# A planned step order, start-up work, the r selection and the weight layout of a one-core recurrence + MLP kernel

## Chip, cores and metric

The kernel runs on one core of one Trainium2 chip. The metric is device time of one execution in microseconds (us), lower is better; the time before is the median of three runs, 318.76 us (314.11 to 320.25).

## What is computed

A linear recurrence over 768 tokens for 4 batches x 8 heads with a 40 x 40 state each, then a two-layer MLP on the 3072 tokens (320 = 8 heads x 40):

```python
for t in range(S):                                   # S = 768, per batch and head
    y[:, :, t] = np.einsum('bhd,bhde->bhe', rt, state)
    Sa = np.einsum('bhde,bhe->bhd', state, at)
    state = state * wt[:, :, None, :] - np.einsum('bhd,bhe->bhde', Sa, bt) \
            + np.einsum('bhd,bhe->bhde', vt, kt)
x = y.transpose(0, 2, 1, 3).reshape(B * S, H * D)    # 3072 x 320
out = np.maximum(x @ w_in, 0.0) ** 2 @ w_out         # 320 -> 2048 -> 320
```

## The kernel before

The recurrence is taken in chunks of L = 64 tokens. A *group* g is one chunk of one pair of batches, so there are 12 x 2 = 24 groups of 128 rows (2 batches x 64 tokens) by 320 columns (8 heads x 40, often padded to 64 each). Group g needs the state that group g - 2 left, so two chains run interleaved. Everything is written in steps; each step is one or several instructions on one engine. A group's steps, with the names that the profile's tiles carry:

- Loads on SP (L289, L302): W, K, B, A, V each as two DMAs of 64 x 8 x 40 floats, R as one DMA of 128 rows of 1280 bytes. Three buffers of each.
- Decay sums: LN (ACT, LNW), LO (POOL, LLO, the low half of a split in two bf16), CS and CE (PE, L323, L336, L340), EXN and EXE (ACT), GLM (POOL).
- Scaling: KBS0, KBS1 (POOL, KB), AS (POOL, A), RC (POOL, RB, a cast of r), VC0, VC1 (POOL, VM, a cast of v into two of four blocks) and VZ0, VZ1 (POOL memsets of the other two).
- Transposes on PE with a copy out of PSUM: KT/KTE (L384, L388), AT/ATE (L394, L406), RT/RTE (L401, L410). RT is the *r selection*: r comes in as rows of eight tokens, and 16 matmuls against pieces of the identity put token u of each eight into every eighth PSUM column.
- The chunk: EB and its mask EBE (DVE, L433), XV + X0 (x, L444, L452), the negated copies UA, UB (ACT, UZ, L457), COR (L466), MA, MB (ACT, VM, L471), the state update ST, STE, SX, SXE (L481 to L504), VT, VTE (L511, L515), CP, CPE (L429, L433), YC + YS (y, L525, L533), YE (DVE).
- The MLP: XT, XTE (transpose), then for each half of the 2048 hidden units U (L561, 64-row matmuls for the last 64 of the 320 inputs), UX and UY (L570) into one PSUM tile hp, RL (ACT relu, L575), SQ (DVE square, L579, tile GT), and down-projections D0 to D3 (L588, tile fo), OE (ACT, L593), OST (SP, two stores of 64 rows, L599).

`Plan` (L37) sets the order. It is a list scheduler at build time: every step has an engine, a guessed duration, dependencies, a shape `mode` on PE (R: 64- or 40-row operands, M: whole 128 x 128, C: 64-column outputs) and a place `g * PERIOD + PLACE[name]`. At each turn it takes, over the engines, the step that can start first; among the steps of an engine that could start within a small window, the one with the lowest place, PE steps of another mode getting a malus of 1.5. Instructions are then issued engine by engine in that order, and on the chip each engine works its own queue in order. PSUM is handed out in the plan: three one-bank buffers S, one two-bank buffer each D (cs, eb, cp) and HP (both halves hp0, hp1), one F (fo).

The constants (identity ID, triangles TI, TE, MASK, selectors SELB, BM, I2) and the zero pads are written ahead of all steps: DVE and POOL memset whole tiles. The weights are loaded by four POOL DMAs with a cast to bf16, ahead of all steps on POOL: WIN as 2 x 128 rows and 128 rows from 192 on (so that input rows 192 to 255 are there twice), WOUT as rows of 320 floats:

```python
nc.gpsimd.dma_start(out=V(WOUT, 0, [(DM, 16), (1, DM)]),
                    in_=moe_w_out.rearrange("(j p) f -> p j f", p=128))
```

Hidden unit 128 * blk + p is thus column p of block blk, a contiguous 128 columns of WIN.

Of the kernel before, what the change touches and what calls it, by code (L numbers as in the profile page):

```python
# [7 lines left out]
FP32 = mybir.dt.float32  # L8
# [6 lines left out]
PERIOD = 9.3  # L15
PLACE = {
# [10 lines left out]
}  # L27
SWITCH = 0.1
# [3 lines left out]
class Op:  # L32
    __slots__ = ("name", "g", "eng", "dur", "fn", "deps", "mode", "alloc", "frees", "place",
# [3 lines left out]
class Plan:  # L37


    LAG = {"PE": 0.2, "ACT": 0.15, "DVE": 0.15, "POOL": 0.2, "SP": 2.2}  # L40
# [14 lines left out]
    def run(self):  # L55
# [19 lines left out]
        while left:  # L75
            best = None
            for e, cand in avail.items():
                lst = []
                for o in cand:
                    t = max(free[e], o.ready)  # L80
                    if o.alloc:
                        cls, key = o.alloc
                        if (key, o.g) not in held:
                            fr = [x for x in banks[cls] if x is not None]
                            if not fr:
                                continue
                            t = max(t, min(fr))
# [11 lines left out]
            if best is None:  # L99
                raise RuntimeError("no step can start")  # L100
# [37 lines left out]
def kernel(  # L138
# [97 lines left out]
    for t in LNW + LLO + A + RB:  # L236
        nc.gpsimd.memset(t[:], 0.0)
# [400 lines left out]
```

## Time and profile before

| | |
|---|---|
| median of three runs | 318.76 us (314.11 to 320.25) |
| the profiled execution | 317.43 us, of which span 315.7 us |
| PE / its weight loads (PEld) | 271.5 us (86%) / 216.9 us (69%) busy |
| DVE / ACT / POOL | 186.9 (59%) / 149.6 (47%) / 142.4 us (45%) busy |
| DMA | 31.29 MB, mean 99 GB/s; loads and stores 49.5%, weights 5.5% of 16 engines' span |
| chain that ended last | PE 70%, SP's queue 11%, DVE 6%, ACT 5% |
| granted TensorE clock | 0.987 |

The span is the time from the first to the last instruction; the execution's own time has 1.7 us around it. A row of a group view names line, engine, operation, output tile <- input tiles and shape, then busy time and mean ns of one instruction, then idle time of the engine before it and what ended that. A row of a timeline gives start and length in us, then the instruction; in brackets stands how long the engine had been idle and for whom. Matmuls are pipelined and overlap, so their mean ns is not the time that one costs. PEld is the load of the stationary operand, which runs beside the matmuls. DMA rows give the median time from issue to landing.

### The profile page before, as it was taken

To read this page: it belongs to the slowest core of one execution; us is meant where nothing else is said; L and a number is where in the kernel's file an instruction comes from. 1 tells how busy PE (TensorE), PEld (TensorE's weight loads), DVE (VectorE), ACT (ScalarE), POOL (GpSimd) and SP (SyncE) were. 2 spreads that over 40 slices of the span, in tenths; PEclk is the share of its full clock that TensorE was granted. 3 is DMA by queue.
4 is the path that set the end of the run, shared out by engine and by line. 5 is a ranking of instruction groups with operands and counts; after the bars stand their busy time and mean duration, and the time that the engine had idled before them with its cause. 6 is when DMAs were issued, how large, how long until landed. Compare 5 with 4: busy or idle time off the path is not lost.

```text
span 315.7 us, 13625 instructions
## 1 busy us (share of the span) xinstructions
PE 271.5 (86%) x5928; PEld 216.9 (69%) x5928; DVE 186.9 (59%) x288; ACT 149.6 (47%) x265; POOL 142.4 (45%) x259
## 2 busy tenths in 40 slices
PE   0132899599999899999999999999999999999872
PEld 0031678478787578777878778887887787787651
DVE  7420538545583585587566577758665855875620
ACT  2103254255737445665455654565456465453431
POOL 8442576433755354646345733456444562510000
PEclk9999999989999799999999999999999999999999
DMA  5999776677665766666665765657564311001110
GB/s 80 196 182 167 119 119 110 121 111 142 116 141 87 128 121 106 113 129 124 101 119 108 116 125 99 117 100 125 106 117 89 55 36 23 22 5 23 23 23 21
DMA packets 136571, 31.29 MB, mean 99 GB/s; under 512 B 127936, under 2 KB 136128, under 8 KB 136512
## 3 DMA queue, kind: packets, MB, share of 16 engines
q1 hardware_dynamic: 134016, 27.55, 49.5%
q0 software_dynamic: 2496, 2.88, 5.5%
q8 instruction: 46, 0.75, 1.0%
q14 instruction: 13, 0.11, 0.1%
HBM read 29.36 MB, written 3.93 MB: 105 GB/s over the span
## 4 chain that ended last, share of the span: by engine, by line
PE 70%; SPq 11%; DVE 6%; ACT 5%; DMA 3%; issue 3%; POOL 0%; ACTq 0%; POOLq 0%
PE fo L588 17%; PE hp L570 15%; SPq L289 10%; PE hp L561 5%; PE sx L500 3%; PE vt L511 3%; PE kt L384 3%; PE rt L401 3%; DVE GT L579 3%; PE cs L323 2%; PE y L525 2%; ACT RL L575 2%; DMA Wf<-in_w_dram 2%; PE st L481 2%; PE x L444 2%
## 5 line engine op out<-in xcount | busy, mean ns | idle before, releaser
L575 ACT ACTIVATE RL<-hp 128x1024 bf16<-128x1024 f32 x48 | 49.1, 1023 | 63.7 <-PE hp L570 60.8
L588 PE MATMUL fo<-WOUT,GT 128*128 128x320 bf16 x384 | 61.5, 303 | 3.5 <-DVE GT L579 3.1
L356 POOL TENSOR_TENSOR KB<-KBf,EXN 128x320 bf16<-128x320 f32 x48 | 40.8, 870 | 35.6 <-issue 12.3
L570 PE MATMUL hp<-XT,WIN 128*128 128x128 bf16 x768 | 54.4, 223 | 0.0
L570 PEld LDWEIGHTS <-WIN 128*128 128x128 bf16 x768 | 45.4, 100 | 5.6 <-issue 0.4
L588 PEld LDWEIGHTS <-GT 128*128 128x128 bf16 x384 | 34.8, 99 | 17.3 <-DVE GT L579 5.1
L579 DVE TENSOR_TENSOR GT<-RL 128x1024 bf16<-128x1024 bf16 x48 | 37.7, 785 | 12.5 <-ACT RL L575 12.2
L362 POOL TENSOR_TENSOR A<-Af,EXE 128x320 bf16<-128x320 f32 x24 | 20.9, 869 | 38.2 <-issue 21.8
L372 POOL CAST VM<-Vf 64x320 bf16<-64x320 f32 x48 | 23.2, 483 | 27.1 <-issue 15.5
L433 DVE TENSOR_TENSOR CPM<-cp,MASK 128x1024 bf16<-128x1024 f32 x24 | 29.2, 1216 | 4.5 <-PE cp L429 4.5
L433 DVE TENSOR_TENSOR EBM<-eb,MASK 128x1024 bf16<-128x1024 f32 x24 | 29.2, 1217 | 3.2 <-PE eb L429 3.1
L515 DVE COPY VMT<-vt 128x1024 bf16<-128x1024 bf16 x24 | 16.5, 689 | 24.3 <-PE vt L511 24.1
L457 ACT ACTIVATE UZ<-x 64x320 bf16<-64x320 f32 x48 | 20.6, 430 | 13.5 <-PE x L452 13.0
L388 DVE COPY KBT<-kt 128x1024 bf16<-128x1024 bf16 x24 | 16.5, 687 | 15.7 <-PE kt L384 15.5
L329 ACT ACTIVATE EXN<-cs 128x640 f32<-128x640 f32 x24 | 16.8, 700 | 14.6 <-PE cs L323 13.9
L367 POOL CAST RB<-Rf 128x320 bf16<-128x320 f32 x24 | 11.3, 470 | 27.0 <-PE rt L401 11.5
L471 ACT ACTIVATE VM<-x 64x320 bf16<-64x320 f32 x48 | 20.6, 429 | 5.7 <-PE x L466 5.2
L561 PE MATMUL hp<-XT,WIN 64*128 64x128 bf16 x384 | 19.4, 221 | 3.5 <-ACT RL L575 2.2
L315 POOL TENSOR_TENSOR LLO<-LNW 128x320 bf16<-128x320 f32 x24 | 17.8, 742 | 9.1 <-ACT LNW L307 8.4
L406 DVE COPY ART<-ar 128x512 bf16<-128x512 bf16 x24 | 10.0, 419 | 19.2 <-PE ar L394 19.1
L593 ACT ACTIVATE OSB<-fo 128x320 f32<-128x320 f32 x24 | 10.5, 436 | 22.2 <-PE fo L588 22.1
L307 ACT ACTIVATE LNW<-Wf 128x320 f32<-128x320 f32 x24 | 11.2, 466 | 20.1 <-DMA Wf<-in_w_dram 20.0
(81 smaller groups left out, 500.5 us busy)
## 6 DMA issues: line engine op xcount, KB each, us to landing
Wf<-in_w_dram SPq DMA_DIRECT2D x48, 80.0 KB, 3.1
KBf<-in_k_dram SPq DMA_DIRECT2D x48, 80.0 KB, 3.1
KBf<-in_b_dram SPq DMA_DIRECT2D x48, 80.0 KB, 3.2
Af<-in_a_dram SPq DMA_DIRECT2D x48, 80.0 KB, 3.0
Rf<-in_r_dram SPq DMA_DIRECT2D x24, 160.0 KB, 3.4
Vf<-in_v_dram SPq DMA_DIRECT2D x48, 80.0 KB, 3.1
out_dram<-OSB SPq DMA_DIRECT2D x48, 80.0 KB, 2.5
WIN<-in_moe_w_in_dram POOLq DMA_DIRECT2D x3, 512.0 KB, 8.1
```

The source lines that it names most:

```text
L289: nc.sync.dma_start(out=V(dst, off(be), [(40, 8), (1, 40)], 64 * h, 64), in_=tok(src, b0 + be))
L356: nc.gpsimd.tensor_tensor(out=V(kb, 512 * be, [(64, 8), (1, 40)]), in0=V(kbf, 320 * be, [(40, 8), (1, 40)]), in1=V(exn, 320 * be, [(40, 8) ...
L362: nc.gpsimd.tensor_tensor(out=V(at, 0, [(64, 8), (1, 40)]), in0=V(af, 0, [(40, 8), (1, 40)]), in1=V(exe, 0, [(40, 8), (1, 40)]), op=ALU.mult)
L372: nc.gpsimd.tensor_copy(out=V(vm, 512 * be, [(64, 8), (1, 40)], h, 64), in_=V(vf, 0, [(40, 8), (1, 40)], h, 64))
L433: nc.vector.tensor_tensor(out=V(dst, 0, [(64, 16), (1, 64)]), in0=V(psum(key, g), 0, [(64, 16), (1, 64)]), in1=V(MASK, 0, [(0, 16), (1, 64 ...
L457: nc.scalar.activation(out=V(uz, 320 * be, [(1, 320)], 64 * be, 64), in_=V(psum("x", g), 0, [(1, 320)], 64 * be, 64), func=ACTF.Copy, scal ...
L471: nc.scalar.activation(out=V(vm, 512 * be, [(64, 8), (1, 40)], 64 * be, 64), in_=V(psum("x", g), 0, [(40, 8), (1, 40)], 64 * be, 64), func ...
L561: mm(out=V(p, 512 * s + 128 * i, [(1, 128)]), lhsT=WIN[1 + s][64 * s:64 * s + 64, 128 * blk:128 * blk + 128], rhs=xt[64 * s:64 * s + 64, 1 ...
L570: mm(out=V(p, 512 * s + 128 * i, [(1, 128)]), lhsT=WIN[x][:, 128 * blk:128 * blk + 128], rhs=xt[:, 128 * x:128 * x + 128], start=False, st ...
L575: nc.scalar.activation(out=rl[:], in_=psum(f"hp{hf}", g)[:], func=ACTF.Relu)
L579: nc.vector.tensor_tensor(out=gt[:], in0=rl[:], in1=rl[:], op=ALU.mult)
L588: mm(out=p[:, 0:320], lhsT=gt[:, 512 * s + 128 * i:512 * s + 128 * i + 128], rhs=WOUT[:, DM * blk:DM * blk + DM], start=blk == 0, stop=blk ...
```

## The change

Six things are altered; every matmul and every elementwise result stays as it was.

1. *Order.* `PLACE`, `PERIOD`, `SWITCH`, the durations and the lags are other numbers; the first three and last three groups get offsets of their own. The malus for changing the PE shape is `STAY`, almost three periods, and the window is 0.11 for PE and zero for the other engines.
2. *Constants and pads as steps.* The constants, the ACT table load and the zero pads are steps that the plan places. Only the pads are zeroed where the rest is written anyway, on DVE. VZ is left out for the first three groups, whose VM is zeroed whole.
3. *First group.* K and B of group 0 are issued from ACT's queue, its KBS1 runs on DVE.
4. *r selection.* The 16 matmuls write 64 contiguous PSUM columns each, against a reordered identity SEL; the copy RTE reads PSUM with a step of 64 columns instead.
5. *Weights.* POOL's weight DMAs are steps after AS of group 0. WOUT row p holds hidden units 16p to 16p + 15 (20 KB of floats, in two DMAs); accordingly the blocks of WIN are read as every sixteenth column. WIN[2] gets 64 rows by DMA and 64 by a DVE copy from WIN[1].
6. *Store.* One DMA of 128 rows per group.

```diff
-PERIOD = 9.3
+PERIOD = 68.08
 PLACE = {
-    "LW": -40, "LK": -39, "LB": -38.5, "LA": -38, "LR": -37, "LV": -36,
...
+    "EB": -15.21, "LW": -4.79, "CS": -4.71, "OE": -1.57, "LB": -0.39, "UY0": -0.07, "MASK": 2.65, "RL1": 2.77,
...
-SWITCH = 0.1
+FIRST = {
...
+LAST = {
...
+SWITCH = 0.095
+STAY = 192.14
+WINDOW = {"PE": 0.11, "ACT": 0, "DVE": 0, "POOL": 0, "SP": 0}
...
-        o.place = g * PERIOD + PLACE[name]
+        o.place = g * PERIOD + PLACE[name] + (FIRST.get(name, 0) if g < 3 else LAST.get(name, 0) if g >= 21 else 0)
...
-                t0 = min(x[0] for x in lst)
-                d = 0.2 if e == "PE" else 0.05
-                t, o = min((x for x in lst if x[0] <= t0 + d),
-                           key=lambda x: (x[1].place + (1.5 if e == "PE" and x[1].mode != mode else 0), x[1].seq))
+                lim = min(x[0] for x in lst) + WINDOW[e]
+                t, o = min((x for x in lst if x[0] <= lim),
+                           key=lambda x: (x[1].place + (STAY if e == "PE" and x[1].mode != mode else 0), x[1].seq))
...
-    for t in LNW + LLO + A + RB:
-        nc.gpsimd.memset(t[:], 0.0)
-    for t in KB + UZ + STB + VM:
-        nc.vector.memset(t[:], 0.0)
...
+            eng = "ACT" if g == 0 and name in ("LK", "LB") else "SP"
+            q_ = nc.scalar if eng == "ACT" else nc.sync
...
-                nc.gpsimd.tensor_tensor(
+                (nc.vector if g == 0 and be else nc.gpsimd).tensor_tensor(
                     out=V(kb, 512 * be, [(64, 8), (1, 40)]), in0=V(kbf, 320 * be, [(40, 8), (1, 40)]),
...
-                    mm(out=V(p, u, [(64, 8), (8, 8)], 64 * al, 64), lhsT=rb[:, 64 * u:64 * u + 64],
-                       rhs=V(ID, 8 * al, [(16, 4), (64, 2), (1, 8)]), start=True, stop=True)
+                    mm(out=V(p, 64 * u, [(1, 64)], 64 * al, 64), lhsT=rb[:, 64 * u:64 * u + 64],
+                       rhs=SEL[:, 64 * al:64 * al + 64], start=True, stop=True)
...
-            nc.scalar.activation(out=art[:, 512:1024], in_=psum("rt", g)[:], func=ACTF.Copy)
+            nc.scalar.activation(out=V(art, 512, [(8, 64), (1, 8)]), in_=V(psum("rt", g), 0, [(1, 64), (64, 8)]),
+                                 func=ACTF.Copy)
...
-                        mm(out=V(p, 512 * s + 128 * i, [(1, 128)]), lhsT=WIN[1 + s][64 * s:64 * s + 64, 128 * blk:128 * blk + 128],
+                        mm(out=V(p, 512 * s + 128 * i, [(1, 128)]), lhsT=V(WIN[1 + s], blk, [(16, 128)], 64 * s, 64),
...
-                            mm(out=V(p, 512 * s + 128 * i, [(1, 128)]), lhsT=WIN[x][:, 128 * blk:128 * blk + 128],
+                            mm(out=V(p, 512 * s + 128 * i, [(1, 128)]), lhsT=V(WIN[x], blk, [(16, 128)]),
...
-            for be in range(2):
-                r0 = (b0 + be) * T + c * L
-                nc.sync.dma_start(out=out[r0:r0 + L, :], in_=osb[64 * be:64 * be + 64, :])
-        add("OST", g, "SP", (2, 0.4), f, [("OE", g)])
+            dst = out[b0 * T + c * L:b0 * T + c * L + L, :]
+            dst = bass.AP(dst.tensor, dst.offset, [[T * DM, 2], [DM, L], [1, DM]])
+            nc.sync.dma_start(out=dst, in_=osb[:])
+        add("OST", g, "SP", 0.6, f, [("OE", g)], dma=0.7)
...
+    def pads(t, n):
+        return V(t, 40, [(64, n), (1, 24)])
+    for i in range(2):
+        init(f"zL{i}", "DVE", 0.2, lambda i=i: (nc.vector.memset(pads(LNW[i], 8), 0.0), nc.vector.memset(pads(LLO[i], 8), 0.0)))
...
+    for i, (r0, n, p0) in enumerate(((0, 128, 0), (128, 128, 0), (256, 64, 64))):
+        init(f"wi{i}", "POOL", 0.6, lambda i=i, r0=r0, n=n, p0=p0: nc.gpsimd.dma_start(
+            out=WIN[i][p0:p0 + n, :], in_=moe_w_in[r0:r0 + n, :]), ["AS"], dma=n * 0.017)
+    init("wi3", "DVE", 0.65, lambda: nc.vector.tensor_copy(out=WIN[2][0:64, :], in_=WIN[1][64:128, :]), ["wi1"])
+    wo_src = moe_w_out.rearrange("(p j) f -> p (j f)", p=128)
+    for i in range(2):
+        init(f"wo{i}", "POOL", 0.6, lambda i=i: nc.gpsimd.dma_start(
+            out=WOUT[:, 8 * i * DM:8 * (i + 1) * DM], in_=wo_src[:, 8 * i * DM:8 * (i + 1) * DM]), ["AS"], dma=3.3)
...
-    load_weights()
```

How the order moves, on PE in the middle of the program: the first matmul of each step, about half a group. Before:

```order
L511 MATMUL vt_4164<-ID,VM_135 128x128
...
L481 MATMUL st_4174<-VM_135,KB_121 64x40
...
L429 MATMUL eb_4208<-ART_129,KBT_132 128x64
...
L561 MATMUL hp_11_4227<-XT_147,WIN_182 128x128
...
L570 MATMUL hp_11_4227<-XT_147,WIN_181 128x128
...
L500 MATMUL sx_4258<-ID,STB_154 128x128
...
L588 MATMUL fo_4269<-WOUT,GT_152 128x320
...
L429 MATMUL cp_4279<-ART_128,VMT_140 128x64
...
L444 MATMUL x_4296<-VM_136,EBM_134 64x40
...
L588 MATMUL fo_4269<-WOUT,GT_153 128x320
```

Now:

```order
L567 MATMUL hp_10_4019<-XT_115,WIN_142 128x128
...
L541 MATMUL xt_4049<-ID,YB_114 128x128
...
L585 MATMUL fo_4053<-WOUT,GT_119 128x320
...
L508 MATMUL vt_4066<-ID,VM_104 128x128
...
L329 MATMUL ce_4076<-LNW_78,TE 128x320
...
L585 MATMUL fo_4053<-WOUT,GT_120 128x320
...
L380 MATMUL kt_4101<-ID,KB_92 128x128
...
L478 MATMUL st_4114<-VM_104,KB_90 64x40
...
L441 MATMUL x_4148<-VM_105,EBM_103 64x40
...
L426 MATMUL cp_4176<-ART_97,VMT_109 128x64
```

Before, the rows go through the shapes M, C, R, R, M, M, M, R, C, M (six changes); now seven M steps stand in one run, followed by C, C, R (two changes). The whole program had 295 changes of shape on PE and has 195.

On SP at the program's start (W, K, B, A, R, V of the groups 0, 1, ...). Before:

```order
L289 DMA Wf_94<-in_w_dram 64x8x40 x2
L289 DMA KBf_97<-in_k_dram 64x8x40 x2
L289 DMA KBf_97<-in_b_dram 64x8x40 x2
L289 DMA Af_100<-in_a_dram 64x8x40 x2
L302 DMA Rf_106<-in_r_dram 128x1x320
L289 DMA Vf_103<-in_v_dram 64x8x40 x2
L289 DMA Wf_95<-in_w_dram 64x8x40 x2
```

Now:

```order
L284 DMA Vf_72<-in_v_dram 64x8x40 x2
L284 DMA Wf_63<-in_w_dram 64x8x40 x2
L284 DMA Vf_73<-in_v_dram 64x8x40 x2
L284 DMA Wf_64<-in_w_dram 64x8x40 x2
L284 DMA Af_69<-in_a_dram 64x8x40 x2
L284 DMA Vf_74<-in_v_dram 64x8x40 x2
L295 DMA Rf_75<-in_r_dram 128x1x320
L284 DMA KBf_67<-in_k_dram 64x8x40 x2
```

W of the second group (now Wf_64) was the seventh transfer and is the fourth; K and B of the first have left this queue.

On POOL at the start, from the triangles on. Before:

```order
L186 AFFINE_SELECT UE<-ones_b 128x128
L237 MEMSET LNW_109 128x512
...
L237 MEMSET RB_127 128x512
L247 DMA WIN_181<-in_moe_w_in_dram 128x2048
...
L249 DMA WOUT<-in_moe_w_out_dram 128x16x320
L377 MEMSET VM_135 64x8x40 x2
...
L377 MEMSET VM_137 64x8x40 x2
L315 TENSOR_TENSOR LLO_111<-LNW_109 128x8x40
L356 TENSOR_TENSOR KB_121<-KBf_97,EXN_113 128x8x40
```

Now:

```order
L601 AFFINE_SELECT UI<-ones_b 128x128
L365 CAST VM_104<-Vf_72 64x8x40 x2
L308 TENSOR_TENSOR LLO_80<-LNW_78 128x8x40
...
L349 TENSOR_TENSOR KB_90<-KBf_66,EXN_82 128x8x40
L355 TENSOR_TENSOR A_93<-Af_69,EXE_84 128x8x40
L308 TENSOR_TENSOR LLO_81<-LNW_79 128x8x40
L360 CAST RB_95<-Rf_75 128x8x40
L654 DMA WIN_144<-in_moe_w_in_dram 64x2048
...
L654 DMA WIN_142<-in_moe_w_in_dram 128x2048
...
L654 DMA WIN_143<-in_moe_w_in_dram 128x2048
L659 DMA WOUT<-in_moe_w_out_dram 128x2560
```

The memsets and the weight DMAs that stood ahead of the first LLO are gone from there; the weights now stand between the steps of groups 0 to 2.

More of the change, by code (lines that the diff above doesn't have):

```diff
@@ L125, in run @@
             for u in o.users:
-                u.ready = max(u.ready, o.end + (self.LAG[e] if u.eng != e or e == "SP" else 0.06))
+                lag = 0.0 if o.dma is not None or u.eng == e == "PE" else self.LAG[e]
+                u.ready = max(u.ready, o.end + lag)
                 u.nleft -= 1
@@ new lines, with f @@
+    init("ID", "POOL", 0.3, tri_const(ID, ALU.is_equal), ["ones"])
+    init("TI", "DVE", 0.4, f, ["UI"])
+    def f():
+        nc.vector.memset(TE[:], 0.0)
+        for P in H:
+            nc.vector.tensor_copy(out=TE[P, P], in_=UE[P, P])
+    init("TE", "DVE", 0.35, f, ["UE"])
+    def f():
+        for P in H:
+            nc.vector.tensor_copy(out=MASK[P, :], in_=UE[P, P])
+    init("MASK", "DVE", 0.2, f, ["UE"])
+    def f():
+        nc.vector.memset(SELB[:], 0.0)
+        nc.vector.memset(BM[:], 0.0)
+        for h in range(2):
+            nc.vector.memset(SELB[H[h], h:h + 1], 1.0)
+            nc.vector.memset(BM[H[h], h:h + 1], 1.0)
```

233 lines of the change are left out of this document (112 added, 121 removed), and 47 rows, old and new, of tables (FIRST, LAST, PLACE).

## Prediction

> **What bounds the kernel now.** I read the page's busy shares first, then the busy time by stages, which shows where PE stands.
>
> ```profile
> 0.00:72.00 72.00, 42.88 (x759) 33.24 (x760) 33.69 (x63) 23.16 (x43) 38.48 (x76) 0.98 0.82 134
> 72.00:292.00 220.00, 214.13 (x4923) 172.59 (x4922) 145.19 (x213) 118.72 (x212) 103.88 (x183) 0.99 0.53 96
> 292.00:316.00 24.00, 14.46 (x254) 11.07 (x254) 8.03 (x12) 7.72 (x12) 0.00 (x0) 0.97 0.10 22
> 72.00:292.00 220.00, 12.56 (x320) 10.16 (x320) 0.99 0.53 96
> ```
>
> Each windows row gives the stretch, its length, and the busy time of PE, PEld, DVE, ACT and POOL, then granted clock, DMA share and GB/s; the last row is the same for L401 alone. From 72 to 292 us PE is busy 214.13 of 220 us and no engine but its own load port above 66% (DVE), so PE sets the pace. L401 runs 16 matmuls a group, so 320 of them are 20 groups: 11.0 us a group. Before 72 us PE idles 29 us, after 292 us 9.5 us. So there are three terms: the price of a group, the start, the end.
>
> **A group's price.** Matmuls overlap, so I price a step from its first start to the next step's first start (columns: start, us, instruction).
>
> ```profile
> 181.09 0.41 PE L429 MATMUL eb<-ART,KBT 40*128 40x64 bf16 x16
> 181.34 0.39 PE L561 MATMUL hp<-XT,WIN 64*128 64x128 bf16 x8
> 181.66 1.07 PE L570 MATMUL hp<-XT,WIN 128*128 128x128 bf16 x16
> 182.56 0.61 PE L500 MATMUL sx<-ID,STB 128*128 128x128 bf16 x8
> 183.01 1.25 PE L588 MATMUL fo<-WOUT,GT 128*128 128x320 bf16 x8
> 184.19 0.41 PE L429 MATMUL cp<-ART,VMT 40*128 40x64 bf16 x16
> 184.53 0.43 PE L444 MATMUL x<-VM,EBM 128*64 128x40 bf16 x16
> ...
> 186.69 0.43 PE L525 MATMUL y<-KB,CPM 128*64 128x40 bf16 x16
> 187.10 0.41 PE L466 MATMUL x<-UZ,EBM 128*64 128x40 bf16 x16
> 187.54 0.64 PE L401 MATMUL rt<-ID,RB 128*64 128x64 bf16 x16
> 188.11 0.31 PE L323 MATMUL cs<-LNW,TI 64*128 64x320 bf16 x2
> 188.49 0.29 PE L544 MATMUL xt<-ID,YB 128*128 128x128 bf16 x2
> ...
> 191.06 0.43 PE L481 MATMUL st<-VM,KB 128*64 128x40 bf16 x16
> 191.33 0.36 PE L486 MATMUL st<-I,SB 128*40 128x40 bf16 x16
> 191.62 0.41 PE L429 MATMUL eb<-ART,KBT 40*128 40x64 bf16 x16
> ```
>
> PE works in three shapes, in the form before the tile sizes: 64 or 40 rows (64*128, 40*128: "R"), whole (128*128: "M"), 64 or 40 columns (128*64, 128*40: "C"). Equal work costs more where the next step has another shape: L429's 16 take 0.25 before the up-projection L561 (same shape), 0.34 before x (another). A change of shape is thus about 0.095 us, and fo's eight, 1.18 with the change behind them, are 1.09. The order's rows, counted by shape, hold 295 changes in the old program and 195 in the new. In the middle the new order repeats one cycle with 8 changes a group; the old has about 12.
>
> The second edit is the r selection. Its 16 matmuls (L401) take 0.57 us, 0.47 without the change of shape, although they stream 64 columns like eb's (0.25 for 16) and have the form of st's (0.27 for 16). What differs is that they write every eighth PSUM column and read the identity in runs of eight. Both become contiguous: I take 0.26, so 0.2 us a group. The bounds are eb's 0.25 and, if neither access was the cause, the old 0.47. The copy after it (L410, 0.60 us, last row of the next fence) now reads PSUM with a step of 64 columns; no row shows such a read. Below it costs nothing more; above, twice its time, which ACT hides, busy 54% of the middle, since cp uses the result about a cycle later.
>
> The new cycle then sums to: eb and cp 0.50, up-projection 2 x 0.23 and 2 x 0.90, sx, vt and kt 3 x 0.45, ar 0.22, xt 0.17, cs 0.29, ce 0.47, fo 2 x 1.09, x and y with partners 2 x 0.41 (186.69 to 187.10), cor 0.27, st 0.27 + 0.19, rt 0.26, together 9.25; with 8 changes 0.76: **10.0 us**. (cs is 188.11 to 188.49 less a change; ce the 0.56 from L336 to L444 in the next fence, less a change; xt and ar go by sx's 0.056 a matmul; cor by st's 0.27, as its 0.44 here holds a wait.)
>
> ```profile
> 126.65 0.31 PE L336 MATMUL ce<-LNW,TE 128*128 128x320 bf16 x1
> ...
> 126.97 0.10 PEld L340 LDWEIGHTS <-LNW 128*128 128x128 bf16 x1
> 126.99 0.10 PEld L340 LDWEIGHTS <-LLO 128*128 128x128 bf16 x1
> 127.02 0.10 PEld L340 LDWEIGHTS <-LNW 128*128 128x128 bf16 x1
> ...
> 127.21 0.43 PE L444 MATMUL x<-VM,EBM 128*64 128x40 bf16 x16
> ...
> 127.95 1.36 DVE L579 TENSOR_TENSOR GT<-RL 128x1024 bf16<-128x1024 bf16 x1
> ...
> 128.90 0.60 ACT L410 ACTIVATE ART<-rt 128x512 bf16<-128x512 f32 x1
> ```
>
> That is without waits. The present 11.0 holds 9.25 + 0.2 + 12 x 0.095 = 10.6 of work and 0.4 of waits. In the new cycle each wait has cover: between x and cor PE has 2.7 us of other steps against the two UZ copies' 0.86, between cp and y 2.6 us against the mask's 1.23 (both rows in the next part). Where cover fails, PE stands: the GT row shows a square of 1.36 us while POOL ran an A beside it, and fo waited for it. I take 10.2, from 10.0 (no wait) to 10.6 (waits half as long again): 0.8 x 20 = **-16 us** (-20 to -8).
>
> **The start.**
>
> ```profile
> 2.30 1.31 SPq L289 DMA_DIRECT2D KBf<-in_k_dram  x2
> 8.73 7.71 SPq L289 DMA_DIRECT2D Wf<-in_w_dram  x2
> 11.12 2.35 POOL L377 MEMSET VM<- 64x320 bf16 x6 [2.51 <-DVE VM L239]
> 13.56 0.72 POOL L315 TENSOR_TENSOR LLO<-LNW 128x320 bf16<-128x320 f32 x1
> 20.78 1.23 DVE L433 TENSOR_TENSOR EBM<-eb,MASK 128x1024 bf16<-128x1024 f32 x1 [0.85 <-PE eb L429]
> 27.05 0.47 ACT L307 ACTIVATE LNW<-Wf 128x320 f32<-128x320 f32 x1 [10.95 <-DMA Wf<-in_w_dram]
> 30.34 0.86 ACT L457 ACTIVATE UZ<-x 64x320 bf16<-64x320 f32 x2
> L588 PE MATMUL fo<-WOUT,GT x384: 296/299/474, 50.5 to 311.4; 128*128 128x320 bf16 x192
> Wf<-in_w_dram SPq DMA_DIRECT2D x48, 80.0 KB, 3.1
> Rf<-in_r_dram SPq DMA_DIRECT2D x24, 160.0 KB, 3.4
> out_dram<-OSB SPq DMA_DIRECT2D x48, 80.0 KB, 2.5
> q1 hardware_dynamic: 134016, 27.55, 49.5%
> q0 software_dynamic: 2496, 2.88, 5.5%
> ```
>
> The first group's LLO stands until 13.56, since POOL first issues the weights and runs the VM memsets, which wait for DVE's pads. Then UZ of group 0, whose mask is done at 22.0, stands until 30.34: PE and ACT have the second group's LNW queued ahead, which waits for a W that SP could not issue past the choked queue (7.71 us for a pair) until the weights were in. In the new program POOL starts with UE, ID, UI and the VC casts, the weights come after AS of group 0 and later, and SP issues V, W, V, W. W of group 0 is SP's second pair, its last DMA issued near 3.0 (the first row: a pair in 1.31), lands 3.1 later, and LLO can start near 6.7. From there to the end of EBM were 8.45 us: 15.2; UZ near 15.5, not 30.3. The weights: q0 took 5.5% of 315.7 = 17.4 us of all 16 DMA engines, q1 (loads and stores) 156.3 us or 6.5 a group. Three groups and the weights are 37 us of DMA, some 2 less with 64 rows of WIN copied on chip and WOUT in long rows, so the first fo comes near 35, not 50.5. Both marks move 15 us; the POOL-to-DVE move of pads, K and B of group 0 on ACT's queue (ACT has nothing else until W lands) and KBS1 on DVE lie inside these marks. What is late next: the WIN2 copy stands on DVE's queue ahead of XT and STB and waits for WIN1; I count it in the 35. With the cheaper steps of the first four groups (4 x 0.6) I take **-17 us**. Bounds: -8, if PE is fed no sooner than the DMA work allows and gains only in the first 30 us; -24, if the 29 idle us fall to 5.
>
> **The end.** The new order puts down-projections of the group before between the last halves, where PE now stands 9.5 us: **-3** (0 to -5). The store becomes one DMA of 160 KB. The r load of that size and row length lands in 3.4 us against 2.5 of a half store, and one issue of 0.6 goes: +0.3. But its destination now has 2 as its outermost dimension, where every transfer of before has 64, 128 or 16. If that spreads it over two engines:
>
> ```profile
> 280.00:300.00 20.00, 17.90 (x397) 14.93 (x396) 13.48 (x19) 9.41 (x17) 1.49 (x2) 1.00 0.08 19
> ```
>
> In this stretch only two groups' stores run: 0.08 x 20 us of 16 engines, 12.8 engine-us a group, 6.4 on two instead of 0.8: +5 at the end. I take the middle, **+2.5**. [...]
>
> **Sum.** 315.7 - 16 - 17 - 3 + 2.5 = 282.2 of span; the profiled run took 317.43, 1.7 more: **284 us**. The median of the runs shown, 318.76, is 0.4% above that run, so nothing is added for it.
>
> **Rivals.**
> [...]
> *The store paces the loads.* If two engines carry each store, they have 6.5 - 0.8 + 6.4 = 12.1 us a group, above PE's 10.2. Three groups by 35 us, 21 more at 12.1, and 25 for the last group's chain give 314; at 10.5, if store packets run faster on a quiet memory, 280 and nothing lost. Between them near 298, with the 1.7 near 299. For it: every group needs loads. Against: three buffers of lead, and the r load, as long, lands as fast as the others.
> *The order doesn't hold.* The steps are placed by assumed durations and lags; if each engine's queue slips, PE waits as in the first 72 us now. If the middle costs its high 10.6 and start and end gain the low 8 and 0: 315.7 - 8 - 8 + 2.5 + 1.7 = 304. For it: DVE's share of the middle rises from 66% to 71%, and each queue is fixed. Against: the covers above are over twice the work they cover.
>
> **Chances.** The forecast, 272 to 295: 0.62. The store as pace: 0.16. Order slips: 0.14. Strided weights: 0.08, nearly all above 325. The range leaves out the strided case and little else: **266 to 308**, the low end from the terms' far ends (-20, -24, -5, +0.3 give 268.7) and a little, the high from 304 and half of the store case above 299. A measurement of this kernel tells about 2% from no change: faster below 312.4, slower above 325.1. Faster 0.87, same 0.05 (the far ends of the store and of the slipping order), slower 0.08.
>
> **What the new profile would show.** the r selection (L397 now) at 0.26 us for its 16, not 0.47; first fo near 35 us; UZ of group 0 near 15.5; in the middle 10.0 to 10.5 us a group by the same matmul count; L567's loads still every 56 ns; the store's landing, 2.5 to 3 us or 6 and more. Wrong would be: a pitch of L567 above 60 ns, PE waiting for Wf, KBf or Vf in the middle, or a first fo after 43.

## The result, and the profile after

The changed kernel takes 300.3 us (median of 4 runs, 297.71 to 303.04) beside 317.52 us for the kernel before on the same chip. The ratio is 0.946, 95% interval 0.932 to 0.961: 17 us faster, where 33 were forecast. The execution that left the profile is the longest of the four, 303.04 us with a span of 301.3. Ratios leave out slow executions, those over 1.5% above the fastest of their kernel, and two profiles are of such executions, this one (the median of the other three is 299.34 us) and that of the kernel with one store and plain weights (301.88, the others 297.97), so some 0.14 of their 10.94 us a group below may belong to the execution and not to the kernel.

From the page of the changed kernel, the span, engine shares, queue q1 and the chain that ended last, by engine and by line:

```profile
span 301.3 us, 13557 instructions
...
PE 265.5 (88%) x5928; PEld 224.5 (75%) x5928; DVE 185.0 (61%) x300; ACT 147.5 (49%) x265; POOL 131.9 (44%) x245
...
q1 hardware_dynamic: 131184, 27.21, 48.7%
...
PE 62%; DMA 16%; ACT 7%; SPq 6%; issue 4%; POOL 1%; DVE 1%; ACTq 0%; POOLq 0%
PE hp L567 16%; PE fo L585 13%; DMA Wf<-in_w_dram 10%; SPq L284 5%; PE hp L558 4%; DMA out_dram<-OSB 4%; ACT RL L572 3%; PE sx L497 3%; PE cs L316 2%; PE kt L380 2%; PE vt L508 2%; PE cp L426 2%; PE eb L426 2%; PE x L463 2%; PE x L441 2%
```

The chain of the kernel before, by engine:

```profile
PE 70%; SPq 11%; DVE 6%; ACT 5%; DMA 3%; issue 3%; POOL 0%; ACTq 0%; POOLq 0%
```

PE still has most of the chain, but 16% of it, 3% before, is now time that the chain spends in a transfer: 10% in loads of W and 4% in stores. One undisturbed cycle of the changed kernel, from the timeline of PE (start, us, instruction):

```profile
131.09 0.61 PE L508 MATMUL vt<-ID,VM 128*128 128x128 bf16 x8
...
134.86 0.46 PE L558 MATMUL hp<-XT,WIN 64*128 64x128 bf16 x8
135.25 1.22 PE L567 MATMUL hp<-XT,WIN 128*128 128x128 bf16 x16
136.31 0.61 PE L497 MATMUL sx<-ID,STB 128*128 128x128 bf16 x8
...
138.13 0.42 PE L397 MATMUL rt<-SEL,RB 128*64 128x64 bf16 x16
138.48 0.41 PE L426 MATMUL eb<-ART,KBT 40*128 40x64 bf16 x16
...
141.40 0.61 PE L508 MATMUL vt<-ID,VM 128*128 128x128 bf16 x8
```

From vt to vt is 10.31 us, where the prediction summed 10.0. The r selection is as forecast: 138.13 to 138.48 is 0.35, less 0.095 for the change of shape 0.26. The up-projection is not: L567's 16 matmuls take 1.06 us (135.25 to 136.31), 66 ns each against 56 before, and L558's eight take 0.39.

That is a clean cycle. What groups really cost, a table from the traces shows: the start of the sixteenth down-projection matmul (L585, L588 before) of groups 0, 5, 19 and 23, the price of a group as the time from group 5 to group 19 over 14, and the span. "Plain" are WIN's blocks as contiguous columns and WOUT loaded as rows of 320 floats, "strided" the change's form of both.

| kernel | g0 | g5 | g19 | g23 | a group | span |
|---|---|---|---|---|---|---|
| before | 55.5 | 119.9 | 273.3 | 311.4 | 10.96 | 315.7 |
| changed (one store, strided) | 51.8 | 111.9 | 265.0 | 294.1 | 10.94 | 301.3 |
| two stores, strided | 53.1 | 107.0 | 251.6 | 280.8 | 10.33 | 285.1 |
| one store, plain | 50.8 | 112.4 | 265.5 | 292.9 | 10.94 | 300.1 |
| two stores, plain | 51.9 | 108.3 | 253.0 | 280.4 | 10.34 | 284.8 |
| two stores, plain, old r selection | 49.9 | 108.6 | 250.3 | 278.1 | 10.12 | 282.5 |
| two stores, plain, four OSB | 51.5 | 108.1 | 247.5 | 274.9 | 9.96 | 279.3 |
| two stores, strided, four OSB | 57.0 | 109.3 | 253.9 | 283.1 | 10.33 | 287.4 |
| one store, strided, four OSB | 54.3 | 112.1 | 257.7 | 286.9 | 10.40 | 294.1 |
| before, strided alone | 54.7 | 118.6 | 277.5 | 317.2 | 11.35 | 321.6 |

The changed kernel gains 8.0 us by group 5, nothing at all in the fourteen groups that follow (10.94 for 10.96), 9.0 from group 19 to 23 (38.1 becomes 29.1), and gives 2.9 back after the last matmul group (4.3 becomes 7.2). So of the forecast's two large places, the start and the middle, the middle is where nothing came.

Why, the waits of ScalarE and its timeline say. The two longest waits for transfers in the changed kernel (us in total, times, longest):

```profile
ACT OSB L590 <- DMA out_dram<-OSB: 23.6, 8, 5.1
ACT LNW L300 <- DMA Wf<-in_w_dram: 23.3, 9, 5.6
```

Around one of the eight stands, ScalarE, SyncE and PE, from the timeline of the changed kernel:

```profile
144.38 0.44 ACT L590 ACTIVATE OSB<-fo 128x320 f32<-128x320 f32 x1 [1.08 <-PE st L478]
150.72 0.57 SPq L596 DMA_DIRECT2D out_dram<-OSB  x1
156.82 0.44 ACT L590 ACTIVATE OSB<-fo 128x320 f32<-128x320 f32 x1 [3.18 <-DMA out_dram<-OSB]
163.50 0.58 SPq L596 DMA_DIRECT2D out_dram<-OSB  x1
169.62 0.44 ACT L590 ACTIVATE OSB<-fo 128x320 f32<-128x320 f32 x1 [5.08 <-DMA out_dram<-OSB]
170.08 0.88 ACT L454 ACTIVATE UZ<-x 64x320 bf16<-64x320 f32 x2
171.01 0.43 PE L463 MATMUL x<-UZ,EBM 128*64 128x40 bf16 x16 [1.94 <-ACT UZ L454]
```

Up to 151 us the lines' own counts are these (form, count, first and last start):

```profile
L590 ACT ACTIVATE OSB<-fo x9: 419/437/438, 52.2 to 144.4; 128x320 f32<-128x320 f32 x9
...
L596 SPq DMA_DIRECT2D out_dram<-OSB x8: 569/573/1208, 60.6 to 150.7; - x8
```

The copy at 144.38 is the ninth and the store at 150.72 the eighth, so the store at 163.50 is that of the copy at 144.38: it left 19.1 us behind its copy, since it stands in SyncE's queue behind the loads of later groups. From group 6 to 16 the k-th store leaves 13 to 19 us after the k-th copy. Then it is under way for another 6, as the chain through this place has it (start, us):

```profile
163.50 6.04 DMA out_dram<-OSB
```

The eleventh copy, at 169.62, needs that buffer: OSB has two. ScalarE stands 5.08 us for it, the UZ copies stand behind it in ScalarE's queue, and PE stands 1.94 us for UZ. A buffer is held about 16 + 6 = 22 us, and two cycles are 20.6.

All eight waits for OSB stand between 153 and 246 us. Of the nine for W, only these three come after group 5 (111.9 us), 1.3 us together:

```profile
112.27 0.47 ACT L300 ACTIVATE LNW<-Wf 128x320 f32<-128x320 f32 x1 [0.67 <-DMA Wf<-in_w_dram]
122.41 0.47 ACT L300 ACTIVATE LNW<-Wf 128x320 f32<-128x320 f32 x1 [0.48 <-DMA Wf<-in_w_dram]
132.81 0.47 ACT L300 ACTIVATE LNW<-Wf 128x320 f32<-128x320 f32 x1 [0.17 <-DMA Wf<-in_w_dram]
```

### The profile page after: what moved, and what is told of

Read it like the earlier page. It is cut to its first block, busy times and chain, and to the rows that moved or that the text cites. A ratio compares the mean times of both kernels' runs of the same rounds, so it can differ in the third digit from the quotient of the medians.

```text
span 301.3 us, 13557 instructions
## 1 busy us (share of the span) xinstructions
PE 265.5 (88%) x5928; PEld 224.5 (75%) x5928; DVE 185.0 (61%) x300; ACT 147.5 (49%) x265; POOL 131.9 (44%) x245
## 3 DMA queue, kind: packets, MB, share of 16 engines
q10 hardware_dynamic: 2112, 0.33, 0.7%
## 4 chain that ended last, share of the span: by engine, by line
PE 62%; DMA 16%; ACT 7%; SPq 6%; issue 4%; POOL 1%; DVE 1%; ACTq 0%; POOLq 0%
PE hp L567 16%; PE fo L585 13%; DMA Wf<-in_w_dram 10%; SPq L284 5%; PE hp L558 4%; DMA out_dram<-OSB 4%; ACT RL L572 3%; PE sx L497 3%; PE cs L316 2%; PE kt L380 2%; PE vt L508 2%; PE cp L426 2%; PE eb L426 2%; PE x L463 2%; PE x L441 2%
## 5 line engine op out<-in xcount | busy, mean ns | idle before, releaser
L585 PE MATMUL fo<-WOUT,GT 128*128 128x320 bf16 x384 | 61.6, 305 | 1.0 <-DVE GT L576 1.0
L567 PE MATMUL hp<-XT,WIN 128*128 128x128 bf16 x768 | 62.1, 236 | 0.0
L567 PEld LDWEIGHTS <-WIN 128*128 128x128 bf16 x768 | 54.6, 151 | 3.7 <-issue 0.6
L576 DVE TENSOR_TENSOR GT<-RL 128x1024 bf16<-128x1024 bf16 x48 | 34.8, 726 | 26.1 <-ACT RL L572 26.0
L585 PEld LDWEIGHTS <-GT 128*128 128x128 bf16 x384 | 35.8, 100 | 13.4 <-DVE GT L576 1.4
L365 POOL CAST VM<-Vf 64x320 bf16<-64x320 f32 x48 | 21.6, 451 | 11.1 <-DMA Vf<-in_v_dram 8.8
L300 ACT ACTIVATE LNW<-Wf 128x320 f32<-128x320 f32 x24 | 11.2, 465 | 23.3 <-DMA Wf<-in_w_dram 23.3
L558 PE MATMUL hp<-XT,WIN 64*128 64x128 bf16 x384 | 22.1, 235 | 0.0
L468 ACT ACTIVATE VM<-x 64x320 bf16<-64x320 f32 x48 | 20.6, 429 | 2.7 <-PE x L463 2.1
L338 ACT ACTIVATE EXE<-ce 128x328 f32<-128x328 f32 x24 | 10.6, 444 | 22.0 <-PE ce L333 20.0
L489 DVE TENSOR_TENSOR STB<-st,GLM 128x640 bf16<-128x640 f32 x22 | 18.1, 824 | 4.2 <-PE st L483 4.2
L501 DVE COPY SB<-sx 128x640 bf16<-128x640 bf16 x22 | 10.8, 491 | 15.0 <-PE sx L497 15.0
```

What stands on the lines that cost most here:

```text
L365: nc.gpsimd.tensor_copy(out=V(vm, 512 * be, [(64, 8), (1, 40)], h, 64), in_=V(vf, 0, [(40, 8), (1, 40)], h, 64))
L468: nc.scalar.activation(out=V(vm, 512 * be, [(64, 8), (1, 40)], 64 * be, 64), in_=V(psum("x", g), 0, [(40, 8), (1, 40)], 64 * be, 64), func ...
L489: nc.vector.tensor_tensor(out=V(stb, 0, [(128, 8), (64, 2), (1, 40)]), in0=V(psum("st", g), 0, [(40, 8), (0, 2), (1, 40)]), in1=V(glm, 0, ...
L558: mm(out=V(p, 512 * s + 128 * i, [(1, 128)]), lhsT=V(WIN[1 + s], blk, [(16, 128)], 64 * s, 64), rhs=xt[64 * s:64 * s + 64, 128 + 128 * s:2 ...
L567: mm(out=V(p, 512 * s + 128 * i, [(1, 128)]), lhsT=V(WIN[x], blk, [(16, 128)]), rhs=xt[:, 128 * x:128 * x + 128], start=False, stop=i == 3 ...
L576: nc.vector.tensor_tensor(out=gt[:], in0=rl[:], in1=rl[:], op=ALU.mult)
```

## The experiments

Ratios are to the kernel before on the same chip. The first four were planned around the rival on record, that the store paces the loads.

**Two stores a group.** The single store becomes two of 64 rows again, all else as changed.

```diff
-            dst = out[b0 * T + c * L:b0 * T + c * L + L, :]
-            dst = bass.AP(dst.tensor, dst.offset, [[T * DM, 2], [DM, L], [1, DM]])
-            nc.sync.dma_start(out=dst, in_=osb[:])
+            for be in range(2):
+                r0 = (b0 + be) * T + c * L
+                nc.sync.dma_start(out=out[r0:r0 + L, :], in_=osb[64 * be:64 * be + 64, :])
```

> The changed kernel with one edit: each group's output leaves in two DMAs of 64 rows, as before the change, in the same place of the order. Theory A (the 128-row store runs on two DMA engines, because its destination's outermost dimension is 2; it delays the loads behind it): OSB no longer waits for an earlier store (23.6 us of such waits now), LNW's waits for Wf fall from 23.3 us to about 10, the end shortens by about 3 us, and the time falls by 8 to 13 us to about 289. Theory B (the waits for Wf come from SP's order and its blocked queue, not from the store's engines): only the end gains, about 297, and the extra issue of 0.6 us a group may cost some of that.

286.84 us (286.68 to 288.83), ratio 0.909 (0.903 to 0.914). Against the changed kernel that is 13.5 us by the medians and 12 by the ratios (0.946 - 0.909, of 316.6), so the single store costs 12 to 13.5 us. Two rows of this kernel's page, and two of ScalarE's waits:

```profile
q1 hardware_dynamic: 131904, 27.22, 53.3%
...
out_dram<-OSB SPq DMA_DIRECT2D x48, 80.0 KB, 2.4
```

```profile
ACT LNW L300 <- DMA Wf<-in_w_dram: 20.3, 8, 6.5
...
ACT OSB L590 <- DMA out_dram<-OSB: 2.1, 4, 0.6
```

q1 has 720 packets more than in the changed kernel, for the same bytes. In the packet records, the last store of the changed kernel has 128 packets of 1280 bytes and two of 4 bytes, the last two half stores of the kernel before have 128 and 32 together; at 16 a half store and two a whole one, 48 half stores and 24 whole ones differ by 768 - 48 = 720. The kernel before (134016) and the changed kernel (133296, with the 2112 of ScalarE's queue) differ by the same 720, all of them packets of 4 bytes (4992 and 4272). While that last store alone is under way, from 296.4 to 299.4 us, the DMA share is 0.13 of 16 engines, which is two; under the last half stores of the kernel before it is 0.34 to 0.64 (in half microseconds from 313.0 to 314.5). So the single store keeps two engines busy, and takes 6.04 us against 2.4 for a half. Whether the destination's outermost dimension, 2 in the one and 64 in the other, is the reason no run tells apart. The waits for W hardly move (23.3 to 20.3), the waits for OSB go: that spoke for the buffers, not for the loads as I had it.

**Plain weights**, with the single store and with two.

```diff
-    lhsT=V(WIN[1 + s], blk, [(16, 128)], 64 * s, 64),
+    lhsT=WIN[1 + s][64 * s:64 * s + 64, 128 * blk:128 * blk + 128],
...
-    lhsT=V(WIN[x], blk, [(16, 128)]),
+    lhsT=WIN[x][:, 128 * blk:128 * blk + 128],
...
-    wo_src = moe_w_out.rearrange("(p j) f -> p (j f)", p=128)
+    wo_src = moe_w_out.rearrange("(j p) f -> p j f", p=128)
...
-            out=WOUT[:, 8 * i * DM:8 * (i + 1) * DM], in_=wo_src[:, 8 * i * DM:8 * (i + 1) * DM]), ["AS"], dma=3.3)
+            out=V(WOUT, 8 * i * DM, [(DM, 8), (1, DM)]), in_=wo_src[:, 8 * i:8 * i + 8, :]), ["AS"], dma=3.3)
```

> The changed kernel with the weights laid out as before: blocks of 128 contiguous WIN columns, WOUT loaded as rows of 320 floats (two DMAs, at the same places of the order). Theory A (a weight load with a step of 32 bytes is exposed): WIN's loads fall from 151 to 100 ns, 16 matmuls of L567 from 1.05 to 0.90 us and 8 of L558 by 0.06, so 48 x 0.15 + 48 x 0.06 = 10 us less PE work; the shorter WOUT rows cost 1 to 2 us of DMA work at the start; time about 291 to 294. Theory B (PE is not what paces the middle, the loads are): the PE work falls but its waits rise as much, and the time stays within 3 us of 300.

298.7 us (296.75 to 301.88), ratio 0.943 (0.936 to 0.950): within 3 us of 300, as theory B has it.

> Both edits: two stores a group and the old weight layout. If the two costs are separate, the gains add: about 281, near the forecast of 284. If the store paces the loads, the weight edit pays only here: more than the sum of the two alone.

285.33 us (284.0 to 286.54), ratio 0.901 (0.894 to 0.908). On one chip the two differ by 13.4 us (12.6 without the longest execution of the first), the store's price again. The two gains add up, but to 285 and not to 281: plain weights give only 1.6 and 1.5 us, though the pitch is back at 56 ns. Where the rest went, ScalarE's first wait in the kernel with two stores and plain weights says:

```profile
ACT OSB L590 <- DMA out_dram<-OSB: 26.0, 8, 4.7
```

Here, from group 8 to 15, the first of a group's two stores leaves 17 to 20 us after the copy and lands 2.2 later, and two cycles are now only 19.8 (2 x 9.9): the shorter cycle runs into the same two buffers. With strided weights 16 to 17 + 2.4 just fits into 20.6, which is why that kernel waits 2.1 us.

**The single store in the old order**: the first diff reversed, on the kernel before.

> The kernel before with only the store changed: one DMA of 128 rows a group. Theory A (two engines carry it): the last store lands about 3 us later, OSB starts to wait for stores, and the time rises by 3 to 10 us. Theory B (one DMA of 160 KB is as good as two of 80): within 1 us of before, perhaps a little less for the issues saved.

320.23 us (319.28 to 320.53), ratio 1.012 (1.007 to 1.018). Its last down-projection stands at 311.3 us, as before (311.4), its span ends at 318.5: the 3 us are all behind the last matmul. From group 7 to 16 its stores leave 7 to 11 us after their copies, so 11 + 6 fit into two cycles of 11; one copy alone waits for OSB, 5.5 us at 83 us. What the store costs in the middle depends on the order it stands in.

**The order alone**: two stores, plain weights and the old r selection in the new order, with all the start-up work as in the change (points 2 and 3 of the change, and the weight loads as steps).

```diff
-                    mm(out=V(p, 64 * u, [(1, 64)], 64 * al, 64), lhsT=rb[:, 64 * u:64 * u + 64],
-                       rhs=SEL[:, 64 * al:64 * al + 64], start=True, stop=True)
+                    mm(out=V(p, u, [(64, 8), (8, 8)], 64 * al, 64), lhsT=rb[:, 64 * u:64 * u + 64],
+                       rhs=V(ID, 8 * al, [(16, 4), (64, 2), (1, 8)]), start=True, stop=True)
...
```

> The changed kernel with all that isn't order undone: two stores a group, plain WIN blocks, WOUT as 640-byte rows, the old r selection. Left of the change is the searched order with its constants and pads as steps. If the parts add up, this is the 285.3 us of the version with two stores and plain weights, plus the r selection's 24 x 0.21 = 5.0: 290 us, about 27 below the kernel before, and the order is nearly the whole of the gain. Rival: PE waits anyway in the steps around the r selection, and its 5 us hide: 285 to 286.

284.8 us (282.71 to 288.76), ratio 0.899 (0.892 to 0.906). Order and start-up work together are worth 31 us, more than the whole change; the r selection's 5 us do not add, as the rival said. ScalarE waits 12.0 us for OSB here against 26.0 with the new selection: a cycle of 10.12 us leaves the stores more time.

**Four OSB buffers**, with two stores and plain weights, in the same order.

```diff
-    OSB = ring("OSB", 2, 320, FP32)
+    OSB = ring("OSB", 4, 320, FP32)
...
-        osb = OSB[g % 2]
+        osb = OSB[g % 4]
```

> The version with two stores and plain weights, with four OSB buffers for two; nothing else, same order. In that version ScalarE stood 26 us before L590 for a store that had not yet freed its OSB buffer, PE had waits for L322 and L454 behind it, and the 10 us of weight-load time that plain blocks save did not show (285.3 against 286.8 us). Theory: the two OSB buffers, on ScalarE, took those 10 us; with four the copy never waits and PE runs at the price of its own work, 0.36 us a group less than with strided blocks: 276 to 280. Rival: the loads of the next groups pace it, and ScalarE stands before L300 instead: 284 to 286.

281.7 us (280.96 to 282.8), ratio 0.893 (0.886 to 0.899): 3.6 us better, less than the 5 to 9 expected, and the shortest of all. The price of a group falls from 10.34 to 9.96, and between 130 and 245 us PE has no wait. What stays is outside: groups 0 to 5 are no faster (108.1 against 108.3). Its up-projection, beside that of the changed kernel above, from PE's timeline:

```profile
140.27 0.39 PE L558 MATMUL hp<-XT,WIN 64*128 64x128 bf16 x8
140.60 1.07 PE L567 MATMUL hp<-XT,WIN 128*128 128x128 bf16 x16
141.50 0.61 PE L497 MATMUL sx<-ID,STB 128*128 128x128 bf16 x8
```

0.33 and 0.90 us, where strided blocks take 0.39 and 1.06: 2 x (0.06 + 0.16) = 0.44 a group.

**Strided weights alone**, on the kernel before.

```diff
-    lhsT=WIN[1 + s][64 * s:64 * s + 64, 128 * blk:128 * blk + 128],
+    lhsT=V(WIN[1 + s], blk, [(16, 128)], 64 * s, 64),
...
-    lhsT=WIN[x][:, 128 * blk:128 * blk + 128],
+    lhsT=V(WIN[x], blk, [(16, 128)]),
...
-        nc.gpsimd.dma_start(out=V(WOUT, 0, [(DM, 16), (1, DM)]),
-                            in_=moe_w_out.rearrange("(j p) f -> p j f", p=128))
+        nc.gpsimd.dma_start(out=WOUT[:], in_=moe_w_out.rearrange("(p j) f -> p (j f)", p=128))
```

> The kernel before with WIN's blocks read as every sixteenth column and WOUT as 20 KB rows; nothing else. Theory: the longer weight loads stand on PE's path wherever PE sets the pace: 32 matmuls of L570 at 10 ns and 16 half loads at 7 ns more are 0.43 us a group, over 20 groups +8.6, less up to 2 for WOUT that comes sooner: 323 to 326. Rival: something else paces the kernel before by as much, as it did between the two versions with two stores (1.5 us apart): 317 to 319.

323.19 us (322.28 to 324.58), ratio 1.023 (1.017 to 1.029): +7.1, 11.35 us a group for 10.96. Of the two, the theory holds. WIN and WOUT change together here; that WIN is what costs is read from the up-projection above, 0.39 and 1.06 us for 0.33 and 0.90.

**The r selection alone**, on the kernel before: the diff of the order alone reversed, with SEL built ahead of the plan and the copy after it.

```diff
-            nc.scalar.activation(out=art[:, 512:1024], in_=psum("rt", g)[:], func=ACTF.Copy)
+            nc.scalar.activation(out=V(art, 512, [(8, 64), (1, 8)]), in_=V(psum("rt", g), 0, [(1, 64), (64, 8)]),
+                                 func=ACTF.Copy)
```

> The kernel before with the new r selection alone (64 columns of SEL to contiguous PSUM, the strided read moved to the ScalarE copy). Theory: 16 matmuls of 0.47 become 0.26, 0.21 x 24 = 5.0 us, of which the 20 groups that PE paces give 4.2: 312 to 313. Rival: waits in the old order fill the time again: 315 to 317.

315.45 us (312.46 to 317.54, 10 runs), ratio 0.996 (0.992 to 1.000): 0.7 us of the 4 to 5. In the old order PE's waits take most of it back; which one was not followed further.

**One store, four buffers**: the changed kernel with the ring of four alone. It tells the buffers from the loads.

> The changed kernel with four OSB buffers for two, the single store kept; same order. Two ways in which the single store can cost its 13.5 us. Theory one, the buffers: a store on two engines takes so long that ScalarE stands before L590 for a free OSB (23.6 us in the changed kernel, 2.1 in the one with two stores) and the copies and exponentials behind it come late; with four buffers that wait goes: 287 to 291. Theory two, the loads (my rival on record): the two engines that carry the store are late for every load's share on them; buffers behind the store change nothing: 297 to 301.

294.24 us (293.03 to 295.8), ratio 0.930 (0.924 to 0.936), between the two. In the table its price is 10.40 a group against 10.94 with two buffers, and from group 9 to 19 (154.3 to 257.7) 10.3, as with two stores: with the same slow store, the middle is whole again. So in the middle the buffers were it, not the loads. Against the next kernel, which differs by two stores, 5.2 us are left: 2.9 behind the last matmul group (7.2 and 4.3 from g23 to the span's end); the profiles put the rest before group 9 (150.5 and 154.3). No profile has a wait for OSB there in the new order, so the rest is not the buffers'. Group 5 shows it in every row of the table: 111.9 to 112.4 us with one store in the new order, 107.0 to 109.3 with two.

**Strided, two stores, four buffers.**

> Two stores and four OSB buffers with the changed kernel's strided WIN blocks and 20 KB WOUT rows: against the 281.7 us of four buffers with plain weights it differs in the weights alone. Theory: where ScalarE doesn't wait, the longer weight loads show in full in the 15 or 20 groups that PE paces, 0.43 us each: 281.7 + 6.5 to 8.6 less up to 2 of earlier WOUT: 286 to 289. Rival: other waits take them in, as between the two versions with two buffers (1.5 us apart): 282 to 284.

289.0 us (286.57 to 289.5), ratio 0.914 (0.908 to 0.920): 7.3 more than with plain weights (6.7 by the ratios), 10.33 for 9.96 a group. Where nothing else waits, the strided blocks cost what they cost alone on the kernel before, 7 us; beside two buffers they cost 1.5. With strided weights, four buffers bring nothing over two (289.0 and 286.84 us, ratios 0.914 and 0.909, both 10.33 a group): the longer cycle already had room for the stores.

**All but the order**, on the kernel before: strided weights, the new r selection, one store.

> The kernel before with the strided weights and 20 KB rows, the new r selection and the single store, in the old order. Adding up the three alone (+7.1, -0.7, +3.6): 326, slower than before by 10. Rival: the old order has little cover against the loads and stores, as the new order had against the store (13.5 us), so that together they cost more: 332 to 340.

326.69 us (326.03 to 327.99), ratio 1.035 (1.029 to 1.041). The three edits add up, 7.1 - 0.7 + 3.6 over 316 give 326. Without the new order and its start-up work, the other edits make the kernel 3.5% slower.

**Stores on ScalarE's queue**, with two stores, plain weights, four buffers.

```diff
-                nc.sync.dma_start(out=out[r0:r0 + L, :], in_=osb[64 * be:64 * be + 64, :])
+                nc.scalar.dma_start(out=out[r0:r0 + L, :], in_=osb[64 * be:64 * be + 64, :])
```

> The version with plain weights, two stores and four OSB buffers (281.7 us), with its stores issued by ScalarE's queue instead of SyncE's. Theory: SyncE stands 34 us before its stores, waiting for the L590 copy, with the next loads queued behind; moved away, the loads of the groups between 70 and 110 us, where PE still loses 9 us, start earlier: 276 to 280. Rival: those loads wait for their buffers anyway, or come late because the DMA engines are busy: 281 to 283; slower than that if the issuing holds ScalarE up.

283.34 us (281.78 to 285.18), ratio 0.898 (0.891 to 0.904), not faster. Stores now leave 0.5 to 2.1 us after their copies, but group 5 stands at 108.3 as before: the early loads do not wait for SyncE's stores. Two buffers with stores on this queue, where a buffer would be held little longer than the landing, were not run.

## Why the prediction was right and where it was wrong

Faster was right, and the range holds 300.3; the point is 16 us short. The case with a chance of 0.62, 272 to 295, did not come. The time lies where the store rival, with 0.16, had put it, and in the middle for another reason than that rival gave; that the range holds it is in part luck. By its own steps:

**The group's price (-16, from 11.0 to 10.2)** is right as a sum of work and wrong as a time. The cycle of 10.0 without waits was measured at 9.96, in the kernel with plain weights, two stores and four buffers. The changed kernel got 10.94. The difference is two terms: 0.37 for strided blocks (9.96 to 10.33) and 0.6 for ScalarE's stands before OSB (10.33 to 10.94, up to 0.14 of it the execution's). My 0.2 for waits looked at the covers of UZ and of the masks, and not at the copy to OSB that stands ahead of UZ on ScalarE.

**The store (+2.5)** is the step that failed. At the end it was well sized, 4.3 became 7.2 us, +2.9, and the two engines, an "if" in the forecast, show in the DMA share of 0.13. But a store that takes 6 us also holds its buffer 6 us, and I had counted the buffer nowhere; the step's whole price is 12 to 13.5. The rival "the store paces the loads" named the right time (near 299) with the wrong resource: with four buffers the middle runs at 10.3 with the same store. For the 2 to 4 us before group 9 that four buffers do not give back, the loads may still be the reason: one store and two differ there in every profile, no copy waits for OSB there, and no run tells which transfer is late. That stays open.

**Strided weights (0, with 0.08 for a time nearly always above 325)** was wrong on both sides. In the changed kernel a weight load of L567 takes 151 ns on average, with plain blocks 99 (groups by line and form, then the page of the kernel with four buffers):

```profile
L567 PEld LDWEIGHTS <-WIN 128*128 128x128 bf16 x768 | 54.6, 151 | 3.7 <-issue 0.6
```

```profile
L567 PEld LDWEIGHTS <-WIN 128*128 128x128 bf16 x768 | 44.0, 99 | 5.3 <-issue 0.5
```

The pitch goes from 56 to 66 ns, over the 60 that I had named as the sign, and costs 7 us alone. The step that failed is that the sum counted nothing for a step of 32 bytes. The forecast's fence with L340 has loads of 128 columns start every 25 ns, with steps of 4 and 2 bytes, but each took 0.10 us in the same rows: the distance between starts is not the length of a load, and neither step tells what one of 32 bytes costs.

**The r selection (0.47 to 0.26)** was met to the hundredth in place and worth 0.7 us alone in the old order, nothing in the new one with two buffers: some 4 of the 16 us (0.2 in each of 20 groups) were never to be had as long as something else set the pace.

**The start (-17)** was half right. UZ of group 0 starts at 18.85 us, forecast 15.5, before 30.34; but the first down-projection, forecast at 35, starts at 49.79, later than the 43 that I had called wrong. From the timeline of the changed kernel, POOL, SyncE, ScalarE and PE:

```profile
18.85 0.89 ACT L454 ACTIVATE UZ<-x 64x320 bf16<-64x320 f32 x2
20.55 0.60 POOL L654 DMA_DIRECT2D WIN<-in_moe_w_in_dram  x1
21.19 1.28 SPq L284 DMA_DIRECT2D Wf<-in_w_dram  x2
22.33 0.54 POOL L659 DMA_DIRECT2D WOUT<-in_moe_w_out_dram  x1
22.57 6.74 SPq L284 DMA_DIRECT2D KBf<-in_b_dram  x2
33.64 0.47 ACT L300 ACTIVATE LNW<-Wf 128x320 f32<-128x320 f32 x1 [5.62 <-DMA Wf<-in_w_dram]
49.79 2.34 PE L585 MATMUL fo<-WOUT,GT 128*128 128x320 bf16 x16
```

```profile
21.83 11.71 DMA Wf<-in_w_dram
```

The choked queue did not go, it moved: W of the fourth group, issued with the weights, has not landed until 33.6, 11.71 us by the chain, and the pair behind it takes SyncE 6.74 us to issue, as a pair took 7.71 before. I had moved the weights "to later" without asking what is loaded then. But that queue is not the whole of it: between 20 and 50 us PE is busy 26.6 us of the 30. Up to 40 us it works at half pace:

```profile
37.96 1.93 PE L567 MATMUL hp<-XT,WIN 128*128 128x128 bf16 x16
39.68 0.82 PE L497 MATMUL sx<-ID,STB 128*128 128x128 bf16 x8
```

The 16 matmuls take 1.72 us, 107 ns each where the middle has 66, although the page's clock says 1.00 for this stretch. Until 40 us PE's other matmuls of 128 x 128 start 106 to 107 ns apart as well (middle values of every 2 us), and those of the kernel before until 48; from there on 56. My 35 us priced the transfers and put PE's pace at nothing. The "some 2 less" in it was an estimate; the weights' queue fell from 17.4 to 14.2 us of 16 engines (5.5% of 315.7 to 4.7% of 301.3). How much of the 15 us up to 49.79 belongs to the queue and how much to the pace, no run tells. By group 5 the order alone is 11.3 us ahead (119.9 to 108.6), the changed kernel 8.0.

**The end (-3)** was too small: from group 19 to 23 the changed kernel takes 29.1 us for 38.1, of which 4 x 0.8 were in the group's price.

The parts, from runs: order, start-up work and r selection 316.6 to 285.3 (-31, forecast -36), strided weights in the changed kernel's company +1.5 (forecast 0), store +12 to 13.5 (forecast +2.5). The forecast of the order was close as a sum, though its parts were not (start 8 to 11 of 17 by group 5, end more than forecast); the two small edits cost what was lost.

## What to carry to other kernels

Price a store by its buffer as well as by its landing: time from copy to issue, plus time to land, against ring depth times the cycle. Here 16 + 6 over 2 x 10.3 cost 5 to 7.5 us in the middle (299.34 to 294.24 by the runs, 14 x 0.54 by the profiles), and a second buffer pair, or two half stores of 2.4 us each with strided weights, took it away. The time to issue was no constant: with four buffers and the same single store, it grew to 17 to 22 us. An edit's price holds for the bound it meets: strided weights cost 7 us alone, 1.5 beside a buffer wait, and 7 again once that wait was gone, so edits that come together are to be undone one by one and in pairs.

## What the runs showed of the hardware

Behind several stands of PE the records have a granted clock of 0.50. Stretches of the changed kernel around the wait at 171.0 us (stretch, length, busy time of PE, PEld, DVE, ACT, POOL, then the clock, DMA share, GB/s):

```profile
170.00:173.20 3.20, 1.79 (x81) 1.70 (x81) 1.30 (x3) 3.16 (x7) 0.67 (x1) 1.00 0.70 135
173.20:176.60 3.40, 3.40 (x25) 2.82 (x26) 1.79 (x3) 1.52 (x3) 1.43 (x3) 0.50 0.67 111
176.60:180.00 3.40, 3.40 (x70) 2.77 (x70) 1.29 (x3) 1.06 (x3) 1.40 (x2) 0.99 0.51 103
```

The clock was 0.50 for 3.4 us. In the changed kernel from 60 us on, such stretches stand at the waits of 3.0, 1.7 and 1.9 us (at 74.9, 93.6 and 171.0 us) and at neither of the two of 1.1. In the kernel with two stores, plain weights and four buffers one stands behind a wait of 2.5 us (clock 0.53 from 85.6 to 89.2), but none behind one of 2.8 (74 to 78 us, clock 1.00). In the kernel before one stands behind waits of only 0.65 and 0.76 us (clock 0.50 from 106.1 to 109.5). In these stretches PE itself is slower: L567's 16 matmuls take 1.72 us (173.12 to 174.84 in the changed kernel) for 1.06 in the cycle above, fo's eight 2.27 (106.45 to 108.72 in the kernel before) for 1.18. So such a stand cost more than its own length; what decides was not tested.

The starts in the table go with the clock in part: the last long stretch at 0.50 in the start ends at 42.6, 42.7 and 46.5 us in the kernels with g0 at 54.3, 53.1 and 57.0, and in the three with g0 at 51.5, 51.8 and 51.9 the records say 1.00 from 20 to 52 us. The order alone is outside this, with a mean of 0.95 over its first 72 us and g0 at 49.9. The records miss part of it: in the changed kernel matmuls start 107 ns apart before 40 us, where they say 1.00.

A ScalarE copy that reads PSUM with a step of 64 columns (L406) takes 596 ns on average, as the contiguous one did (595): the strided side of the r selection costs nothing there, while on TensorE's side its write and read cost 0.47 against 0.26 us.
